# Fixing the issue order of ScalarE, VectorE and GpSimd in the attention stage of a fused gated-linear-attention and mixture-of-experts kernel

## The chip, the core and the metric

The kernel runs on one core of a Trainium2 chip. The metric is device time in microseconds of one execution; the quoted time before is the median of three runs. Engines are called PE (TensorE), ACT (ScalarE), DVE (VectorE), POOL (GpSimd) and SP (the queue that issues the DMAs). Each engine works through its own queue of instructions in the order in which they were put there.

## The reference

Two stages. The first is gated linear attention over 4 batches, 8 heads, 768 time steps, head dimension 48:

```python
for t in range(S):
    state = f[:, :, t, :, None] * state + einsum('bhd,bhe->bhde', k[:, :, t], v[:, :, t])
    y[:, :, t] = einsum('bhd,bhde->bhe', q[:, :, t], state)
```

with `f` the sigmoid of `f_logit`. Its output, reshaped to `x` of 3072 x 384, goes into a soft mixture of 8 experts: `P = exp(x @ w_gate - max)`, eight rounds of Sinkhorn (divide by row sums, then by column sums) over `P`, and `out = sum over e of P[:, e] * (relu(x @ w1[e]) @ w2[e])`, with `w1` 384 x 1024 and `w2` 1024 x 384 for each expert. All in float32.

## The kernel before

**Numbers.** Matmuls run in fp16 on split operands: each float32 operand is a high half and a low half, and three of the four products are kept. So each matmul is issued three times, and each evacuation has two parts: ACT writes the high half (`hh`, `xh`, `ah`, `sh`, `qh`, `vh`), then DVE or POOL subtracts it from the source and writes the low half (`hl`, `xl`, `al`, `sl`, `ql`, `vl`).

**Attention** is cut into 32 items: 4 batches x 2 halves of the sequence x 4 pairs of heads. One item covers 384 time steps in six chunks of 64. `pre(i)` (L398) loads `q3` (gates, q and k: one DMA, called `q<-in_qkf_dram` in the profile) and `vr`, takes the sigmoid (`ft`, ACT), runs two scans (`r` and `q`, DVE), scales and splits q and k (`kb`: high half on ACT, low half on POOL), and has SP transpose `kb` into `kt` by a DMA. `scores(i)` (L438) does the chunk scores (`aps`, 18 matmuls) and the key-value products (`kvps`, 18), masks and splits the scores (`am`, `ah`, `al`), and chains the states (`ut`, `sh`, `sl`). `outputs(i)` (L482) does `yps` (30 to 36 matmuls) and writes the fp16 pair `xh`, `xl`. After each fourth item `logits(u)` (L510) makes the gate logits of that 384-token unit `u`. Buffers limit how far items overlap: three of `q3`, two each of `kb`, `kt`, `vr`, `ut`, `ah`.

**Experts.** `moe(e, u)` (L317) does one expert for one unit: eight groups of nine `hps` matmuls, evacuated by `hh` and `hl`, then three groups of 24 `yps` matmuls. It is a generator that yields after each matmul, so it can fill PE's time elsewhere. `fill(n)` takes n expert matmuls from a list of 13 pairs (e, u) (`RAW`, 1872 matmuls), whose results `yr` are stored unscaled in DRAM and scaled later, when the Sinkhorn result is known. The loop over items (L600) puts 28 fills, then an item's `yps`, then 28 fills, then the next item's `aps` and `kvps`, from item 4 on: 56 fills for each item. The ten matmuls of Sinkhorn have 22 fills ahead of each. Everything left of the experts follows after that.

**What sets the order.** PE's order is the order of the calls: `mm` (L223) puts a dependency that carries no wait on the matmul before. The order on ACT, DVE, POOL and SP is made by the scheduler of the kernel's framework, which plays the program through with its own estimates of time and a priority; expert evacuations have the better priority `EPRIO`. Three scans are held back by hand (L412).

**PSUM.** Eight banks: three for the experts (`psm`), five for attention: one for `aps`, two for `kvps`, two for `yps`, the logits and Sinkhorn. After attention its five go to the experts (`bank`, L310). `guard` and `verdict` (L527, L564) reduce inputs and intermediates (`xmx`, `wmx`, `qkm`, `vm`) to a flag that tells whether the fp16 halves were wide enough.

Of the kernel before, what the change touches and what calls it, by code (L numbers as in the profile page):

```python
# [205 lines left out]
def fast(ctx, tc, qkf, vbd, wg, w1, w2, out, flag):  # L206
# [15 lines left out]

    def mm(transpose=False, **kw):  # L223
        ins = (nc.tensor.transpose if transpose else nc.tensor.matmul)(**kw)  # L224
# [10 lines left out]
    psm = ctx.enter_context(tc.tile_pool(name="psm", bufs=3, space=PSUM))  # L235
# [33 lines left out]
    def split_w(raw, e, j, k):  # L269
# [3 lines left out]
        if e < 2:  # L273
            nc.scalar.activation(out=raw, in_=raw, func=AF.Copy, scale=WS)
            nc.scalar.activation(out=wh, in_=raw, func=AF.Copy)
            nc.gpsimd.tensor_tensor(out=wl, in0=raw, in1=wh, op=ALU.subtract)
# [33 lines left out]
    def bank(shape, name):  # L310
        n = banks[0]
        banks[0] += 1
        if late and n % 8 >= 3:
            return late[1].tile(shape, F32, name=name, tag="m")
        return psm.tile(shape, F32, name=name, tag="m")

    def moe(e, u, w, mode):  # L317
# [3 lines left out]
        for f in range(FT):  # L321
# [15 lines left out]
            with at(EPRIO):  # L337
                nc.scalar.activation(out=th, in_=ps, func=AF.Relu)  # L338
                held[0] = nc.vector.scalar_tensor_tensor(out=tl, in0=ps, scalar=0.0, in1=th, op0=ALU.max, op1=ALU.subtract)  # L339
# [55 lines left out]
    done = {}  # L395
    tds = cst.tile([R, 32, NC], F32, name="tds")

    def pre(i):  # L398
# [8 lines left out]
        nc.scalar.activation(out=ft[:, 0:HS].rearrange("r (c t) -> r c t", t=C)[:, :, 1:C], in_=fl3[:, :, 1:C], func=AF.Sigmoid)  # L407
# [3 lines left out]
        scan = nc.vector.tensor_tensor_scan(out=r[:, ::-1], data0=ft[:, :0:-1], data1=ind[:, :0:-1], initial=0.0, op0=ALU.mult, op1=ALU.add)  # L411
# [4 lines left out]
        nc.vector.reciprocal(out=pi[:, :, 0], in_=pi[:, :, 0])
        nc.vector.tensor_tensor_scan(out=fl, data0=ft[:, 0:HS], data1=pi.rearrange("r c t -> r (c t)"), initial=0.0, op0=ALU.mult, op1=ALU.add)  # L417
        nc.gpsimd.tensor_tensor(out=td, in0=td, in1=r3[:, :, 0], op=ALU.mult)
        nc.gpsimd.tensor_tensor(out=fl, in0=fl, in1=q, op=ALU.mult)
# [3 lines left out]
        nc.vector.tensor_tensor(out=ql, in0=fl, in1=qh, op=ALU.subtract)  # L423
        km = k.rearrange("r (c t) -> r c t", t=C)
        nc.vector.scalar_tensor_tensor(out=km, in0=km, scalar=KS, in1=r3, op0=ALU.mult, op1=ALU.mult)
        for h in range(2):
            rs = slice(64 * h, 64 * h + D)
            cs = slice(64 * h, 64 * h + C)
            nc.scalar.activation(out=kb[rs, 0, :, cs], in_=km[rs], func=AF.Copy)  # L429
            nc.gpsimd.tensor_tensor(out=kb[rs, 1, :, cs], in0=km[rs], in1=kb[rs, 0, :, cs], op=ALU.subtract)  # L430
# [1 line left out]
        nc.sync.dma_start_transpose(out=kt, in_=kb.rearrange("r n c s -> r (n c) s"))
# [3 lines left out]
        return kb, kt, qh, ql, vh, vl, td

    def scores(i, st):  # L438
        b, hf, p = i // 8, (i // 4) % 2, i % 4
        kb, kt, qh, ql, vh, vl, td = st  # L440
        kh, kl = kb[:, 0], kb[:, 1]
        cs = [slice(c * C, (c + 1) * C) for c in range(NC)]
# [5 lines left out]
        ins = nc.vector.scalar_tensor_tensor(out=am, in0=aps, scalar=AS, in1=mask[:, None, :].to_broadcast([128, NC, C]), op0=ALU.mult, op1=ALU.mult)
# [17 lines left out]
        if hf:
            nc.gpsimd.tensor_scalar(out=ut[:, 0, :], in0=carry[p], scalar1=1.0, scalar2=1.0, op0=ALU.mult, op1=ALU.mult)
        for c in range(NC - hf):
            kv = kvps[c // 3][:, c % 3, :]
            un = ut[:, c + 1, :] if c < NC - 1 else carry[p]  # L470
            if hf or c:
                nc.vector.scalar_tensor_tensor(out=un, in0=ut[:, c, :], scalar=td[:, c:c + 1], in1=kv[0:R], op0=ALU.mult, op1=ALU.add)  # L472
            else:
# [2 lines left out]
        nc.gpsimd.tensor_tensor(out=ut[:, c0:], in0=ut[:, c0:], in1=td[:, c0:, None].to_broadcast([R, NC - c0, 96]), op=ALU.mult)
        nc.scalar.activation(out=sh[:, c0:], in_=ut[:, c0:], func=AF.Copy, scale=SS)  # L477
        nc.vector.scalar_tensor_tensor(out=sl[:, c0:], in0=ut[:, c0:], scalar=SS, in1=sh[:, c0:], op0=ALU.mult, op1=ALU.subtract)  # L478

        return ah, al, shw, slw, c0  # L480

    def outputs(i, st, sc):  # L482
# [20 lines left out]
        for si, so, kt in pcs:  # L503
            nc.scalar.activation(out=xh[so, kt, :], in_=yps[si], func=AF.Copy, scale=YS * XS)  # L504
# [185 lines left out]
```

## Time and profile before

| | |
|---|---|
| median of 3 runs | 1737.86 us (1737.3 to 1743.14) |
| profiled execution | 1742.68 us, of which its span is 1740.9 us |
| PE busy | 1622.4 us of the span |
| DVE, ACT, POOL busy | 794.9, 472.3, 213.1 us |
| mean granted PE clock | 0.983 |

A row of the profile names the line, the engine, the operation and `out<-in`. Lines are those of the kernel before; L224 is the helper through which every matmul goes, so matmuls are told apart by their tiles. A "busy" PE counts a matmul from its start to its modelled end, so neighbouring matmuls overlap in it. "PEclk" is the granted clock as a share of full speed.

### The profile page before, as it was taken

To read this page: it belongs to the slowest core of one execution; us is meant where nothing else is said; L and a number is where in the kernel's file an instruction comes from. 1 tells how busy PE (TensorE), PEld (TensorE's weight loads), DVE (VectorE), ACT (ScalarE), POOL (GpSimd) and SP (SyncE) were. 2 spreads that over 40 slices of the span, in tenths; PEclk is the share of its full clock that TensorE was granted. 3 is DMA by queue.
4 is the path that set the end of the run, shared out by engine and by line. 5 is a ranking of instruction groups with operands and counts; after the bars stand their busy time and mean duration, and the time that the engine had idled before them with its cause. 6 is when DMAs were issued, how large, how long until landed. Compare 5 with 4: busy or idle time off the path is not lost.

```text
span 1740.9 us, 27224 instructions
## 1 busy us (share of the span) xinstructions
PE 1622.4 (93%) x11566; PEld 1003.7 (58%) x11566; DVE 794.9 (46%) x1482; ACT 472.3 (27%) x947; POOL 213.1 (12%) x231
## 2 busy tenths in 40 slices
PE   2479898898999999999999999999999999999998
PEld 2246565565665566666666666666666666666665
DVE  8886666666468942235222522243223422223222
ACT  5544444444332221112111311122112211111111
POOL 7663343333100000000000000000000000000000
PEclk9989999999999999999999999999999999999999
DMA  8453343343014610002000200010000100000000
GB/s 196 129 141 99 95 100 96 97 115 74 27 51 159 171 37 1 1 10 64 1 1 1 73 1 1 1 47 27 1 1 19 37 1 1 1 5 24 28 29 29
DMA packets 87956, 86.72 MB, mean 50 GB/s; under 512 B 58768, under 2 KB 71952, under 8 KB 87824
## 3 DMA queue, kind: packets, MB, share of 16 engines
q1 hardware_dynamic: 87824, 84.89, 18.3%
q8 instruction: 92, 1.51, 0.4%
q14 instruction: 40, 0.33, 0.1%
HBM read 61.47 MB, written 12.39 MB: 42 GB/s over the span
## 4 chain that ended last, share of the span: by engine, by line
PE 75%; DVE 9%; DMA 7%; POOL 3%; issue 3%; ACT 2%; SPq 1%; POOLq 0%; ACTq 0%; DVEq 0%
PE yps L224 38%; PE hps L224 36%; DMA q<-in_qkf_dram 6%; DVE r L411 1%; POOL kb L430 1%; DVE hl L339 1%; DVE xl L506 1%; DMA yb<-ys 1%; DVE ql L423 1%; DVE wmx L285 1%; DVE q L417 1%; POOL al L454 1%; PE kvps L224 1%; ACT xh L504 1%; DVE vl L435 1%
## 5 line engine op out<-in xcount | busy, mean ns | idle before, releaser
L224 PE MATMUL yps<-w2h,hl 128*128 128x384 f16 x1536 | 501.4, 326 | 6.1 <-DVE hl L339 5.9
L224 PE MATMUL yps<-w2h,hh 128*128 128x384 f16 x1536 | 501.3, 326 | 4.5 <-DVE hl L339 4.5
L224 PE MATMUL yps<-w2l,hh 128*128 128x384 f16 x1536 | 501.3, 326 | 0.0
L338 ACT ACTIVATE hh<-hps 128x384 f16<-128x384 f32 x512 | 246.7, 488 | 911.2 <-PE hps L224 910.6
L224 PEld LDWEIGHTS <-w1h 128*128 128x128 f16 x3072 | 301.4, 98 | 240.4 <-issue 47.2
L339 DVE SCALAR_TENSOR_TENSOR hl<-hps,hh 128x384 f16<-128x384 f32 x512 | 280.2, 554 | 342.8 <-ACT hh L338 341.7
L224 PEld LDWEIGHTS <-hh 128*128 128x128 f16 x3072 | 300.3, 98 | 195.8 <-issue 1.0
L224 PE MATMUL hps<-xh,w1h 128*128 128x384 f16 x1536 | 339.4, 329 | 43.6 <-DVE hl L339 36.4
L224 PE MATMUL hps<-xh,w1l 128*128 128x384 f16 x1536 | 339.4, 330 | 0.0
L224 PE MATMUL hps<-xl,w1h 128*128 128x384 f16 x1536 | 337.9, 328 | 0.0
L306 DVE SCALAR_TENSOR_TENSOR acc<-yps,pes,acc 128x384 f32<-128x384 f32 x153 | 94.4, 617 | 430.4 <-PE yps L224 430.4
L224 PEld LDWEIGHTS <-hl 128*128 128x128 f16 x1536 | 150.5, 98 | 112.1 <-DVE hl L339 9.8
L224 PEld LDWEIGHTS <-w1l 128*128 128x128 f16 x1536 | 151.4, 99 | 101.4 <-issue 5.0
L430 POOL TENSOR_TENSOR kb<-q,kb 48x384 f16<-48x384 f32 x64 | 64.4, 1006 | 31.6 <-ACT kb L429 29.2
L224 PEld LDWEIGHTS <-kb 112*128 112x128 f16 x576 | 26.6, 110 | 45.5 <-issue 33.0
L411 DVE TENSOR_TENSOR_SCAN r<-ft,ind 112x384 f32<-112x384 f32 x32 | 33.1, 1038 | 37.4 <-ACT ft L407 37.3
L478 DVE SCALAR_TENSOR_TENSOR sl<-ut,sh 112x480 f16<-112x480 f32 (+1 forms) x32 | 25.4, 795 | 49.7 <-ACT sh L477 49.7
L224 PE MATMUL aps<-qh,kb 112*128 112x64 f16 x384 | 26.8, 211 | 22.9 <-ACT qh L422 22.9
L472 DVE SCALAR_TENSOR_TENSOR ut<-ut,tds,kvps 112x96 f32<-112x96 f32 x144 | 44.6, 310 | 5.2 <-PE kvps L224 0.2
L429 ACT ACTIVATE kb<-q 48x384 f16<-48x384 f32 x64 | 33.3, 520 | 49.8 <-PE aps L224 33.8
L224 PE MATMUL yps<-qh,sh 112*128 112x64 f16 x176 | 33.8, 202 | 9.2 <-ACT sh L477 9.2
L224 PE MATMUL yps<-qh,sl 112*128 112x64 f16 x176 | 33.7, 199 | 7.7 <-DVE sl L478 7.7
(130 smaller groups left out, 1118.3 us busy)
## 6 DMA issues: line engine op xcount, KB each, us to landing
q<-in_qkf_dram SPq DMA_DIRECT2D x32, 504.0 KB, 5.1
w1r<-in_w_dram SPq DMA_DIRECT2D x32, 384.0 KB, 3.5
w2r<-in_w_dram SPq DMA_DIRECT2D x32, 384.0 KB, 3.2
vr<-in_vbd_dram SPq DMA_DIRECT2D x32, 288.0 KB, 3.4
ys<-yr SPq DMA_DIRECT2D x39, 192.0 KB, 2.0
yb<-ys SPq DMA_DIRECT2D x13, 576.0 KB, 4.0
out_dram<-acc SPq DMA_DIRECT2D x24, 192.0 KB, 1.9
vs<-in_vbd_dram SPq DMA_DIRECT2D x4, 384.0 KB, 3.5
```

The lines of the kernel that those rows point to most:

```text
L224: ins = (nc.tensor.transpose if transpose else nc.tensor.matmul)(**kw)
L285: ins = nc.vector.tensor_reduce(out=wmx[:, k - 1, 4 * e + j:4 * e + j + 1], in_=wh.rearrange("p a f -> p (a f)"), axis=AX.X, op=ALU.max, a ...
L306: nc.vector.scalar_tensor_tensor(out=a, in0=y, scalar=p, in1=a, op0=ALU.mult, op1=ALU.add)
L338: nc.scalar.activation(out=th, in_=ps, func=AF.Relu)
L339: held[0] = nc.vector.scalar_tensor_tensor(out=tl, in0=ps, scalar=0.0, in1=th, op0=ALU.max, op1=ALU.subtract)
L411: scan = nc.vector.tensor_tensor_scan(out=r[:, ::-1], data0=ft[:, :0:-1], data1=ind[:, :0:-1], initial=0.0, op0=ALU.mult, op1=ALU.add)
L417: nc.vector.tensor_tensor_scan(out=fl, data0=ft[:, 0:HS], data1=pi.rearrange("r c t -> r (c t)"), initial=0.0, op0=ALU.mult, op1=ALU.add)
L423: nc.vector.tensor_tensor(out=ql, in0=fl, in1=qh, op=ALU.subtract)
L429: nc.scalar.activation(out=kb[rs, 0, :, cs], in_=km[rs], func=AF.Copy)
L430: nc.gpsimd.tensor_tensor(out=kb[rs, 1, :, cs], in0=km[rs], in1=kb[rs, 0, :, cs], op=ALU.subtract)
L472: nc.vector.scalar_tensor_tensor(out=un, in0=ut[:, c, :], scalar=td[:, c:c + 1], in1=kv[0:R], op0=ALU.mult, op1=ALU.add)
L478: nc.vector.scalar_tensor_tensor(out=sl[:, c0:], in0=ut[:, c0:], scalar=SS, in1=sh[:, c0:], op0=ALU.mult, op1=ALU.subtract)
```

## The change

The attention item becomes one generator, `item(i)`, in 25 stages. A loop counts steps `g`; at each step every live item runs one stage, oldest first, then a weight load may follow, then about nine fills (56 in six steps). A new item begins every six steps (`STEPS`), with six steps more (`GAP`) between items 3 and 4. Below, "step n of an item" counts from its sigmoid: 0 `ft`; 1 first scan and `vh`; 2 second scan and k; 3 `vl`, q on POOL, `kb` high; 4 `qh`, `kb` low; 5 the transpose; 6 `ql`; 8 `aps` and `kvps`; 9 `am`; 10 `ah` and half of `ut`; 11 the rest of `ut`, and `al`; 12 `ut` on POOL; 14 `sh`; 16 `sl`; 17 `yps`; 18 `xh`; 19 `xl`; and for each fourth item 22 to 25 the logits. The two loads stand four steps ahead of step 0.

`pin` ties each instruction of ACT, DVE and POOL to the one called before it on the same engine, with the same waitless dependency that PE has. It acts from step 24 until attention ends, on the items, on the weights of experts 0 and 1 and on the evacuations of the fills. SP is not pinned.

The experts get four PSUM banks (`psm`), attention four: `yps` has one bank, the logits share the bank of `aps`, Sinkhorn takes the `kvps` pair. Loads of expert weights stand at fixed steps: expert 0 at steps 16 to 30, expert 1 at 36 to 50. Fills begin at step 38, where item 4's `aps` stands, so 56 of them come ahead of item 5's `aps` where 28 did. `guard` becomes a generator that is called piece by piece during expert 3, and its `xmx` reductions are tied behind an expert evacuation.

```diff
+STEPS = 6
 FILL = 56
+GAP = 6
...
+    last, fixed = {}, [False]
+
+    def pin(ins):
+        engine = ins.ins.engine
+        if fixed[0]:
+            if engine in last:
+                behind(ins, last[engine])
+            last[engine] = ins
+        return ins
...
-    psm = ctx.enter_context(tc.tile_pool(name="psm", bufs=3, space=PSUM))
+    psm = ctx.enter_context(tc.tile_pool(name="psm", bufs=4, space=PSUM))
...
-        if late and n % 8 >= 3:
+        if late and n % 8 >= 4:
...
-                nc.scalar.activation(out=th, in_=ps, func=AF.Relu)
+                pin(nc.scalar.activation(out=th, in_=ps, func=AF.Relu))
...
-    def pre(i):
+    def item(i):
...
+        yield from wait(4)
+        pin(nc.scalar.activation(out=ft[:, 0:HS]..., func=AF.Sigmoid))
...
+            pin(nc.scalar.activation(out=kb[rs, 0, :, ks], in_=km[rs], func=AF.Copy))
+        yield
...
+            pin(nc.gpsimd.tensor_tensor(out=kb[rs, 1, :, ks], in0=km[rs], in1=kb[rs, 0, :, ks], op=ALU.subtract))
+        yield
...
         nc.sync.dma_start_transpose(out=kt, in_=kb.rearrange("r n c s -> r (n c) s"))
...
-        yps = psa.tile([128, HS], F32, name=f"yps_{i}", tag="y")
+        yps = psa.tile([128, HS], F32, name=f"yps_{i}", tag="y", bufs=1)
...
-        ps = psa.tile([128, HS], F32, name=f"lps{u}", tag="y")
+        ps = psa.tile([128, HS], F32, name=f"lps{u}", tag="a", bufs=1)
...
         for u in range(U):
-            nc.vector.tensor_reduce(out=xmx[:, u, :], in_=xt[u][0], axis=AX.X, op=ALU.max, ...)
+            yield
+            behind(nc.vector.tensor_reduce(out=xmx[:, u, :], in_=xt[u][0], axis=AX.X, op=ALU.max, ...), held[0])
...
+    loads = {}
     for j in range(4):
-        loads[6 + j // 2] = loads.get(6 + j // 2, []) + [(1, 1, j), (1, 2, j)]
+        loads[16 + 2 * j], loads[24 + 2 * j] = (0, 1, j), (0, 2, j)
+        loads[36 + 2 * j], loads[44 + 2 * j] = (1, 1, j), (1, 2, j)
+    begin = {STEPS * i + (GAP if i >= 4 else 0): i for i in range(4 * U)}
+    live, g, filling = [], -4, False
+    while live or g < max(begin):
+        fixed[0] = g >= STEPS * 4
+        if g + 4 in begin:
+            live.append(item(begin[g + 4]))
+        for it in list(live):
+            if next(it, it) is it:
+                live.remove(it)
+        if g in loads:
+            e, k, j = loads[g]
+            if len(ws[e][k - 1]) == j:
+                ws[e][k - 1].append((load_w1 if k == 1 else load_w2)(e, j))
+        if g >= STEPS * 3 + 20:
+            fill(FILL * (g % STEPS + 1) // STEPS - FILL * (g % STEPS) // STEPS)
+        g += 1
+    fixed[0] = False
-    late.append(ctx.enter_context(tc.tile_pool(name="psb", bufs=5, space=PSUM)))
+    late.append(ctx.enter_context(tc.tile_pool(name="psb", bufs=4, space=PSUM)))
+    checks = guard()
```

ACT in the middle of attention, before. `ft_113<-q_12` is the sigmoid of item 12, `kb_112<-q_10` the high half of k of item 10, `hh` are expert evacuations:

```order
L422 ACTIVATE qh_1667<-q_10_1654 112x384
L504 ACTIVATE xh_959<-yps_1406 96x384
L407 ACTIVATE ft_113<-q_12_2051 112x6x63
L409 ACTIVATE tds<-q_12_2051 112x6
L338 ACTIVATE hh_0_2_1473<-hps_0_2_1399 128x384
L338 ACTIVATE hh_0_3_1487<-hps_0_3_1477 128x384
L338 ACTIVATE hh_0_4_1501<-hps_0_4_1491 128x384
L429 ACTIVATE kb_112<-q_10_1654 48x6x64 x2
```

The same engine at the same place now:

```order
L442 ACTIVATE kb_118<-q_9_1378 48x6x64 x2
L372 ACTIVATE yr_0_0_1610<-yps_0_0_1531 128x384
L476 ACTIVATE ah_1618<-am_1597 128x384
L446 ACTIVATE qh_1624<-q_9_1378 112x384
L515 ACTIVATE xh_1042<-yps_1638 32x384 x3
L421 ACTIVATE ft_113<-q_10_1583 112x6x63
L423 ACTIVATE tds<-q_10_1583 112x6
```

Before, the sigmoid of item i+2 stood ahead of the k of item i; now an item's k stands ahead of the next item's sigmoid.

SP at that place, before. The first transpose is item 9's, the second item 10's:

```order
L432 DMA_TRANSPOSE kt_146<-kb_118 128x12x112
L402 DMA q_12_2051<-in_qkf_dram 112x1152
L404 DMA vr_1852<-in_vbd_dram 128x576
L432 DMA_TRANSPOSE kt_144<-kb_112 128x12x112
L402 DMA q_13_2242<-in_qkf_dram 112x1152
```

And now, from item 8's transpose to item 9's and the load behind it:

```order
L451 DMA_TRANSPOSE kt_144<-kb_112 128x12x112
L415 DMA q_11_1770<-in_qkf_dram 112x1152
L417 DMA vr_1772<-in_vbd_dram 128x576
L451 DMA_TRANSPOSE kt_146<-kb_118 128x12x112
L373 DMA ys_105<-yr_0_0_1610 128x384
L415 DMA q_12_1987<-in_qkf_dram 112x1152
```

In both, the load for item i+3 stands right behind the transpose of item i; what moved is ACT's sigmoid that uses it.

PE at the end of Sinkhorn, now. `sk_c` are its last two column sums, `yps_7_2` the last of the 1872 fills, `hps_3_0` the first matmul of the expert stage behind it:

```order
L236 LDWEIGHTS hh_7_7_6697
L236 MATMUL yps_7_2_6779<-w2l_3_639,hh_7_7_6697 128x384
L236 MATMUL sk_c_6798<-sk_cs,onesf 128x8
L236 MATMUL sk_c_6828<-sk_cs,onesf 128x8
L236 LDWEIGHTS w1h_0_710
L236 MATMUL hps_3_0_6849<-xh_2639,w1h_0_710 128x384
```

Before, its last column sum stood among fills:

```order
L224 LDWEIGHTS hl_7_6_6706
L224 MATMUL yps_7_1_6773<-w2h_3_1120,hl_7_6_6706 128x384
L224 MATMUL sk_c_6767<-sk_cs,onesf 128x8
L224 LDWEIGHTS hh_7_6_6705
L224 MATMUL yps_7_1_6773<-w2l_3_1121,hh_7_6_6705 128x384
```

The fills now run out earlier: 16 stand ahead of the last column sum but one, none ahead of the last.

More of the change, by code (lines that the diff above doesn't have):

```diff
@@ L416, in pre @@
[L416 to L419, printed above, removed]
+        pin(nc.vector.tensor_scalar(out=pi[:, :, 0], in0=r3[:, :, 0], scalar1=T_MIN, scalar2=None, op0=ALU.max))
+        pin(nc.vector.reciprocal(out=pi[:, :, 0], in_=pi[:, :, 0]))
@@ L423, in pre @@
[L423 to L430, printed above, removed]
+        pin(nc.scalar.activation(out=qh, in_=fl, func=AF.Copy))
@@ L436, in pre @@
[L436 to L440, printed above, removed]
+        yield
+        pin(nc.vector.tensor_tensor(out=ql, in0=fl, in1=qh, op=ALU.subtract))
+        yield from wait(2)
         kh, kl = kb[:, 0], kb[:, 1]
-        cs = [slice(c * C, (c + 1) * C) for c in range(NC)]
         aps = psa.tile([128, NC, C], F32, name=f"aps_{i}", tag="a", bufs=1)
@@ L503, in outputs @@
         for si, so, kt in pcs:
-            nc.scalar.activation(out=xh[so, kt, :], in_=yps[si], func=AF.Copy, scale=YS * XS)
+            pin(nc.scalar.activation(out=xh[so, kt, :], in_=yps[si], func=AF.Copy, scale=YS * XS))
+        yield
         for si, so, kt in pcs:
-            ins = nc.vector.scalar_tensor_tensor(out=xl[so, kt, :], in0=yps[si], scalar=YS * XS, in1=xh[so, kt, :], op0=ALU.mult, op1=ALU.subtract)
-        if i == 3:
-            done[5] = done[6] = ins
-    def logits(u):
-        xh, xl = xt[u]
-        fill(FILL // 4)
-        ps = psa.tile([128, HS], F32, name=f"lps{u}", tag="y")
+            pin(nc.vector.scalar_tensor_tensor(out=xl[so, kt, :], in0=yps[si], scalar=YS * XS, in1=xh[so, kt, :], op0=ALU.mult, op1=ALU.subtract))
+        if p < 3:
+            return
+        yield from wait(3)
+        ps = psa.tile([128, HS], F32, name=f"lps{u}", tag="a", bufs=1)
         n = 0
@@ L518, in logits, with wait @@
                 n += 1
+        yield
         lt = ap.tile([2 * NE, HS], F32, name=f"lt{u}", tag="am")
-        nc.scalar.activation(out=lt, in_=ps[0:2 * NE], func=AF.Copy, scale=1.0 / (XS * GS))
-        fill(FILL // 4)
-        ps2 = psa.tile([128, TT, 2 * NE], F32, name=f"lps2{u}", tag="y")
+        pin(nc.scalar.activation(out=lt, in_=ps[0:2 * NE], func=AF.Copy, scale=1.0 / (XS * GS)))
+        yield
+        ps2 = psa.tile([128, TT, 2 * NE], F32, name=f"lps2{u}", tag="a", bufs=1)
         for t in range(TT):
             mm(transpose=True, out=ps2[:, t, :], in_=lt[:, t * 128:(t + 1) * 128], identity=identf[0:2 * NE, 0:2 * NE])
-        nc.vector.tensor_reduce(out=lg[:, u * TT:(u + 1) * TT, :], in_=ps2.rearrange("p t (n e) -> p t e n", n=2), axis=AX.X, op=ALU.add)
+        yield
+        pin(nc.vector.tensor_reduce(out=lg[:, u * TT:(u + 1) * TT, :], in_=ps2.rearrange("p t (n e) -> p t e n", n=2), axis=AX.X, op=ALU.add))
+    def wait(n):
+        for _ in range(n):
+            yield
     def guard():
@@ L554, in guard @@
         for u in range(U):
-            nc.vector.tensor_reduce(out=xmx[:, u, :], in_=xt[u][0], axis=AX.X, op=ALU.max, apply_absolute_value=True)
+            yield
+            behind(nc.vector.tensor_reduce(out=xmx[:, u, :], in_=xt[u][0], axis=AX.X, op=ALU.max, apply_absolute_value=True), held[0])
+        yield
         nc.vector.tensor_reduce(out=g[:, 4:5], in_=xmx.rearrange("p u k -> p (u k)"), axis=AX.X, op=ALU.min)
@@ L642, in fast @@
                     largest(*early.pop(0))
-            if (e, u) == (3, 0):
-                guard()
+                if e == 3 and n % 24 == 12:
+                    next(checks, None)
+            if (e, u) == (3, U - 1):
+                for _ in checks:
+                    pass
             if (e, u) == (NE - 1, 1):
```

108 lines of the change are left out of this document (49 added, 59 removed).

## Prediction

> **What bounds the kernel now.** I read the page first, then a table of stretches, then the waits of the worst stretch, then one of its stalls in order of time.
>
> ```profile
> span 1740.9 us, 27224 instructions
> ```
>
> The stretches are the lead-in without fills, the first items with fills, steady attention, and (Sinkhorn and the start of the late experts left out) the rest. Columns: length, then busy us and instructions of PE, weight loads, DVE, ACT and POOL, then PE's granted clock, DMA share and GB/s.
>
> ```profile
> 0.00:67.60 67.60, 21.14 (x312) 19.44 (x313) 53.05 (x101) 35.63 (x68) 43.99 (x45) 1.00 0.75 183
> 67.60:120.30 52.70, 35.14 (x293) 21.31 (x293) 49.41 (x72) 31.43 (x58) 41.35 (x36) 0.84 0.49 121
> 120.30:452.00 331.70, 288.35 (x2976) 193.02 (x2975) 210.21 (x447) 146.06 (x321) 123.64 (x147) 0.95 0.39 96
> ...
> 620.00:1741.00 1121.00, 1115.09 (x6864) 671.29 (x6861) 355.41 (x601) 209.60 (x411) 0.00 (x0) 1.00 0.05 16
> ```
>
> From 620 us on PE is never idle except for the tail of 5.9 us, and the change leaves that part's work alone. What can be won lies before: PE is idle for 46.5, 17.6 and 43.4 us in the first three stretches, and in the second and third its clock is also cut, by 0.16 x 52.7 + 0.05 x 331.7 = 25 us of time. In steady attention no other engine is full (DVE 210 of 332 us, ACT 146, POOL 124), so PE waits for order, not for work. The waits of 120.3 to 452 us (total, times, longest):
>
> ```profile
> ACT ft L407 <- DMA q<-in_qkf_dram: 45.3, 19, 4.4
> ACT sh L477 <- POOL ut L476: 43.2, 19, 3.7
> DVE r L411 <- ACT ft L407: 34.5, 15, 3.6
> PE hps L224 <- DVE hl L339: 31.5, 10, 6.4
> ```
>
> PE itself waits for few things: mostly an expert bank whose `hl` is late. Behind that, ACT sits at the sigmoid of an item whose load has not landed, 19 times, and DVE at the scan behind it. One stall, in order of time:
>
> ```profile
> 201.52 1.37 SPq L432 DMA_TRANSPOSE kt<-kb  x1
> ...
> 203.62 0.68 ACT L477 ACTIVATE sh<-ut 112x576 f16<-112x576 f32 x1 [3.25 <-POOL ut L476]
> 203.87 0.38 SPq L402 DMA_DIRECT2D q<-in_qkf_dram  x1
> ...
> 206.83 0.49 ACT L338 ACTIVATE hh<-hps 128x384 f16<-128x384 f32 x1
> ...
> 208.18 0.52 ACT L407 ACTIVATE ft<-q 112x378 f32<-112x378 f32 x1 [0.86 <-DMA q<-in_qkf_dram]
> ```
>
> ```profile
> 210.53 0.48 PE L224 MATMUL hps<-xh,w1h 128*128 128x384 f16 x1 [6.42 <-DVE hl L339]
> ```
>
> ACT waits 3.25 us at `sh`, then does other attention rows; the expert's `hh` gets its turn only at 206.83, and PE has no bank for 6.42 us. The load is issued behind the transpose and used 4.3 us later.
>
> **The loop that the order makes.** The rows shown of ACT and SP before close a circle: the transpose of item i, then the load of i+3 behind it on SP, then its sigmoid on ACT, then, behind that on ACT, the k of item i+1, its low half on POOL, and the transpose of i+1. Its links:
>
> ```profile
> q<-in_qkf_dram SPq DMA_DIRECT2D x32, 504.0 KB, 5.1
> ```
>
> ```profile
> L407 ACT ACTIVATE ft<-q 112x378 f32<-112x378 f32 x20 | 10.4, 518 | 41.0 <-DMA q<-in_qkf_dram 40.9
> ```
>
> ```profile
> L429 ACT ACTIVATE kb<-q 48x384 f16<-48x384 f32 x44 | 22.9, 521 | 38.0 <-PE aps L224 29.3 <-issue 8.1
> ```
>
> ```profile
> L430 POOL TENSOR_TENSOR kb<-q,kb 48x384 f16<-48x384 f32 x44 | 41.5, 942 | 26.8 <-ACT kb L429 25.2
> ```
>
> That is 1.37 (issue of the transpose) + 5.1 + 0.52 + 0.52 + 2 x 0.94 = 9.4 us, plus up to three `hh` between sigmoid and k, each of which waits for its nine matmuls (1.46 us by the price below): 9.4 to 13.8 us an item. Now the prices of PE and the ends of the stage:
>
> ```profile
> 634.96 11.70 PE hps L224 x72
> ```
>
> ```profile
> 298.20:309.57 11.37, 11.37 (x126) 7.75 (x125) 5.99 (x14) 4.29 (x9) 5.15 (x7) 1.00 0.51 129
> ```
>
> ```profile
> 67.62 0.48 PE L224 MATMUL hps<-xh,w1h 128*128 128x384 f16 x1 [0.74 <-ACT xh L504]
> ```
>
> ```profile
> L448 DVE SCALAR_TENSOR_TENSOR am<-aps,mask x32: 525/548/559, 20.7 to 463.8; 128x384 f32<-128x384 f32 x32
> ```
>
> A fill costs 11.70 / 72 = 0.1625 us. From 298.20 to 309.57, the starts of two `aps`, PE runs a whole item with its 56 fills without a gap: 11.37 us, so the item's own matmuls cost 2.27. From the first fill to the last item's `am` are 396.2 us, in which PE has 1484 fills (241.2), 27 items (61.3) and seven logits of about 1.1 (7.7): 310 us of work. **86 us are lost there**, 61 of them idle and 25 to the clock; by the item that is 14.7 us for 11.4 of work.
>
> **The change, part by part.** *The loop is cut.* ACT now takes an item's k before the next sigmoid, and the load issued behind the transpose of item i (its step 5) is needed at its step 18, 13 steps later. A step is 9.3 fills, 1.5 us, so the 5.1 us of landing have 20 us of cover. The 45.3 us of ACT at the sigmoid go, and the 34.5 of DVE behind them. `sh` stands two steps after POOL's `ut`, so the 43.2 us go too, if POOL keeps up.
>
> *What is late next.* Loads for each item are 210.21 / 23 = 9.1 us on DVE (8.8 without `xmx`), 6.4 on ACT and 5.4 on POOL against PE's 11.4, so nothing is full, but DVE has little slack. Each engine now waits in a fixed place: `sl` (step 16) is queued behind the `hl` of step 15, and PE's `yps` (step 17) waits for it; behind `yps` stand all fills.
>
> ```profile
> L339 DVE SCALAR_TENSOR_TENSOR hl<-hps,hh 128x384 f16<-128x384 f32 x72 | 38.2, 546 | 9.4 <-ACT hh L338 9.0
> ```
>
> ```profile
> L478 DVE SCALAR_TENSOR_TENSOR sl<-ut,sh 112x576 f16<-112x576 f32 (+1 forms) x24 | 17.0, 708 | 49.3 <-ACT sh L477 49.3
> ```
>
> An `hl` ends about 1.1 us behind PE's step (0.49 of `hh` and 0.55), `sl` takes 0.7, and PE's next step gives 1.5, so `yps` waits 0.3 us at worst from that. [...] The same `ql` in two stretches (67.6 to 120.3, then 135 to 460), and POOL's weight rows that run in the first:
>
> ```profile
> L423 DVE TENSOR_TENSOR ql<-q,qh 112x384 f16<-112x384 f32 x5 | 9.1, 1842 | 0.0
> ```
>
> ```profile
> L423 DVE TENSOR_TENSOR ql<-q,qh 112x384 f16<-112x384 f32 x22 | 13.0, 590 | 0.0
> ```
>
> ```profile
> L276 POOL TENSOR_TENSOR w1l<-w1r,w1h 128x768 f16<-128x768 f32 x8 | 13.7, 1720 | 0.8 <-ACT w1h L275 0.8
> ```
>
> 1842 ns beside POOL rows of 1720, 590 otherwise: about a whole POOL row is added. I take one POOL row of k, 0.94 us, lost for each item; the bounds are 0 (PE's own gap-free item) and two such rows, 1.9. By the 590 alone there would be no loss, and the time 23 us lower. [...]
>
> *Expert 1's weights* (steps 36 to 50, eight loads) are pinned ahead of the `hh` of their steps. PE needs 16 steps, 30.3 us; DVE has 2.67 items x 8.8 = 23.5 us, plus up to 8 x 1.72 = 13.8 behind POOL, 37. I take 10 us lost (7 over PE's time, 3 for waits), bounds 4 and 18. Before, this work fell in the stretch with DVE at 49.4 of 52.7 us.
>
> *Lead-in.* Up to the first fill the same rows run on DVE (53 of 67.6 us busy), but item 4 now follows item 3 in place of running among its rows. I take 0; bounds -5 (idle DVE closed) and +8 (item 4's chain from sigmoid to transpose left bare).
>
> *Fourth expert bank.* PE may run three groups, 4.4 us, ahead of an `hl` where it could run two, 2.9. No price of its own: it is the cover for DVE's lag above. One `yps` bank is free by step 19 and needed at 23; the logits share `aps`'s bank with a step between each user. I take nothing for either.
>
> *`xmx`.* Eight rows leave attention for expert 3, where PE is never idle:
>
> ```profile
> L555 DVE TENSOR_REDUCE xmx<-xh 128x3 f32<-128x1152 f16 x8 | 10.8, 1349 | 0.2
> ```
>
> The 0.35 us an item are in the 8.8 above, and cost nothing there.
>
> *Sinkhorn.* Fills run out, since they begin earlier and there are 1872 in both. DVE's own chain of one round, with two `hl` inside:
>
> ```profile
> 514.10 0.15 DVE L92 TENSOR_SCALAR sk_cs<-sk_c 128x8 f32<-128x8 f32 x1
> ...
> 517.02 0.50 DVE L89 TENSOR_REDUCE sk_cs<-pe 128x8 f32<-128x192 f32 x1
> ```
>
> is 3.4 us. 16 fills cover 2.6 of the last round but one, none covers the last: 0.8 + 2.9 (without the two `hl`) is about 3.5 us of new idle PE; bounds 2.5 and 5.
>
> **Clock.** Around the stall above:
>
> ```profile
> 204.00:210.50 6.50, 0.12 (x1) 0.00 (x0) 5.55 (x9) 4.59 (x11) 0.71 (x1) 0.87 0.64 168
> 210.50:217.00 6.50, 6.46 (x53) 4.50 (x53) 5.08 (x13) 2.06 (x4) 2.28 (x3) 0.60 0.02 4
> ```
>
> The clock falls to 0.60 for the stretch behind it. I let all 25 us of clock loss go, since no stall of more than 2 us remains in my sum. [...]
>
> **Sum.** Lost after: 10 + 24.7 items (steps 52 to 200) x 0.94 = 33 of the 86. Gain 53, less 3.5: 49.5 us. The profiled execution took 1742.68 us, 1.8 over its span and 4.8 over the median; 1740.9 - 49.5 = 1691.4 of span, and against the median 1737.86 - 49.5 = **1688.4**.
>
> **Rivals.** *Collisions cost double.* If DVE loses two POOL rows an item (1.9 us) and the weight stretch 10, the loss is 57 and the time 1737.9 - 29 + 3.5 = 1712. For it: DVE at 80% of PE's time, the 1842 ns. Against: `ql` at 590 in steady attention, where POOL was as busy. *Nearly free.* Losses of 0.1 an item and 4 us: 1737.9 - 80 + 3.5 = 1662. *The weights eat it.* Weight rows pinned ahead of `hh` also wait for their DMA (two raw buffers); with 18 us there, 1.9 an item and 8 us of lead-in, the gain is 86 - 65 - 8 - 3.5 = 9.5: 1728, no change that counts from there on. *Slower: the transposes.* `kvps` (step 8) must have `kt`, eight steps after a sigmoid that is now tied to PE's progress. PE's eight steps last 8 x 1.5 + 2.3 = 14.4 us; sigmoid 0.52, two scans at the row of one,
>
> ```profile
> L417 DVE TENSOR_TENSOR_SCAN q<-ft,pi 112x384 f32<-112x384 f32 x20 | 19.5, 973 | 0.5
> ```
>
> 1.95, three smaller rows and the scaling of k at little more than a third scan, 1.2, `kb` 0.52 + 1.88, and the transpose,
>
> ```profile
> kt<-kb SPq DMA_TRANSPOSE x32, 3.5
> ```
>
> come to 9.6. If each of the five changes of engine waits 1.6 us behind rows of other items, `kt` lands 3.2 us late, PE stops at every `kvps`, and the loss is 10 + 24.7 x (3.2 + 0.94) = 112: 1768. It decides once an item loses 3.3 us in all. For it: DVE and ACT rows that start only behind `hh` or `hl`. Against: those trail PE by about 1 us, and PE's stop gives the chain time. That the pins do nothing is excluded by the rows of ACT shown.
>
> **Chances.** Forecast 0.55 (1672 to 1702 on its own), double collisions 0.20, nearly free 0.10, gain eaten 0.07, slower 0.08. A measurement of this kernel can tell about 0.5% from no change: 1729 to 1747. Faster 0.85, same 0.07, slower 0.08. The range, 1662 to 1728, holds the first two cases and most of the third.
>
> **Right or wrong.** Right: in steady attention ACT's wait at the sigmoid for its load is gone, `aps` starts come 12 to 13 us apart, and the last `am` starts near 415 us against 463.8 (28 more fills, 4.6 us, stand ahead of it now); PE has one idle of about 3 us at the last `sk_c`. Wrong: `ql` and `sl` above 1.2 us on average (collisions), PE waiting at `kvps` for a DMA (transposes), first fill after 75 us (lead-in), or ACT waiting for `w1r` or `w2r` (weights).

## The result, and the profile after

The changed kernel took 1682.68 us in the median (four runs, 1681.21 to 1683.65), the kernel before 1737.58 beside it: a ratio of 0.9678, 95% interval 0.9655 to 0.9701. 1688.4 had been forecast. The profiled execution took 1681.94 us.

```profile
span 1680.2 us, 27209 instructions
```

The items give marks that both kernels share. The table of stretches of the kernel before, cut at the first fill, at the `am` of item 8 and at that of item 31 (columns as in the prediction):

```profile
67.60:143.60 76.00, 50.69 (x442) 31.75 (x442) 63.29 (x99) 38.96 (x76) 48.36 (x44) 0.85 0.48 122
143.60:463.80 320.20, 284.61 (x2967) 190.75 (x2965) 201.73 (x431) 142.54 (x310) 118.69 (x141) 0.96 0.37 91
463.80:620.00 156.20, 150.87 (x992) 90.46 (x989) 121.42 (x252) 45.53 (x83) 2.06 (x2) 0.99 0.40 117
```

The same stretches of the changed kernel:

```profile
66.20:120.00 53.80, 50.83 (x494) 33.30 (x492) 46.65 (x80) 35.40 (x68) 39.02 (x38) 0.93 0.66 157
120.00:399.70 279.70, 272.08 (x2956) 183.51 (x2955) 222.07 (x445) 146.80 (x321) 141.65 (x149) 1.00 0.49 108
399.70:560.00 160.30, 149.29 (x959) 88.58 (x956) 118.45 (x245) 44.40 (x81) 2.06 (x2) 0.98 0.39 115
```

The first of the three holds 28 more fills than before (4.6 us) and the last 28 fewer. With that, the first gave 76.0 + 4.6 - 53.8 = 26.8 us, the second 40.5, and the third took 160.3 + 4.6 - 156.2 = 8.7 back. With 1.4 in the lead-in and 0.7 behind 560 us that is the 60.7 by which the spans differ. In the second stretch PE's idle time fell from 35.6 to 7.6 us and its clock went from 0.96 to 1.00. The medians lie 5.8 us closer than the spans, since the profiled execution of before was about 5 us over its median and that of the changed kernel 0.7 under.

Two waits of that stretch in the kernel before, against which the experiments below are measured (total us, times, longest):

```profile
ACT ft L407 <- DMA q<-in_qkf_dram: 38.2, 17, 4.1
PE hps L224 <- DVE hl L339: 28.3, 9, 6.4
```

What ACT waited for in the second stretch of the changed kernel:

```profile
ACT hh L350 <- PE hps L236: 52.7, 41, 3.0
ACT yr L372 <- issue: 23.8, 10, 3.7
ACT yr L372 <- PE yps L236: 23.3, 13, 3.6
```

The sigmoid's wait for its load and that of `sh` for `ut` (45.3 and 43.2 us in the prediction's somewhat longer stretch) have left the list. ACT now waits for PE, which is how it has to be when PE is the bound. What PE still waits for, from 66 to 400 us:

```profile
PE yps L236 <- DVE sl L495: 5.6, 7, 2.3
PE lps L236 <- DVE am L469: 4.3, 4, 2.0
PE kvps L236 <- DMA kt<-kb: 0.5, 1, 0.5
```

No `hps` waits for a bank any more; small waits for single attention rows on DVE have come in their place.

### The profile page after: what moved, and what is told of

The parts are those of the page before. It is cut to its first block, busy times and chain, and to the rows that moved or that the text cites. A ratio compares the mean times of both kernels' runs of the same rounds, so it can differ in the third digit from the quotient of the medians.

```text
span 1680.2 us, 27209 instructions
## 1 busy us (share of the span) xinstructions
PE 1607.3 (96%) x11566; PEld 995.1 (59%) x11566; DVE 805.3 (48%) x1482; ACT 474.6 (28%) x947; POOL 230.3 (14%) x231
## 4 chain that ended last, share of the span: by engine, by line
PE 86%; DVE 6%; DMA 2%; ACT 2%; issue 2%; POOL 1%; SPq 0%; POOLq 0%; DVEq 0%; ACTq 0%
PE yps L236 43%; PE hps L236 41%; DVE hl L351 1%; PE kvps L236 1%; DVE wmx L297 1%; PE aps L236 1%; PE lps L236 1%; DMA q<-in_qkf_dram 1%; DVE acc L318 1%; DMA w2r<-in_w_dram 1%; DMA yb<-ys 1%; ACT hh L350 1%; DVE vl L438 1%; POOL kb L448 0%; DMA kt<-kb 0%
## 5 line engine op out<-in xcount | busy, mean ns | idle before, releaser
L350 ACT ACTIVATE hh<-hps 128x384 f16<-128x384 f32 x512 | 250.3, 490 | 955.4 <-PE hps L236 954.0
L236 PE MATMUL hps<-xh,w1l 128*128 128x384 f16 x1536 | 335.4, 327 | 0.0
L448 POOL TENSOR_TENSOR kb<-q,kb 48x384 f16<-48x384 f32 x64 | 76.7, 1198 | 16.2 <-ACT kb L442 13.7
L236 PE MATMUL yps<-qh,sl 112*128 112x64 f16 x176 | 33.5, 198 | 13.3 <-DVE sl L495 13.2
L439 POOL TENSOR_TENSOR q<-q 112x384 f32<-112x384 f32 x32 | 39.5, 1234 | 34.6 <-DVE q L433 24.6
L491 POOL TENSOR_TENSOR ut<-ut,tds 112x480 f32<-112x480 f32 (+1 forms) x32 | 39.6, 1237 | 22.6 <-DVE ut L481 11.8
L372 ACT ACTIVATE yr<-yps 128x384 f32<-128x384 f32 x39 | 19.1, 491 | 77.1 <-PE yps L236 48.1
L290 ACT ACTIVATE w2h<-w2r 128x768 f16<-128x768 f32 x24 | 20.2, 843 | 69.9 <-PE yps L236 38.8
```

The costliest lines, as they stand in the source:

```text
L350: pin(nc.scalar.activation(out=th, in_=ps, func=AF.Relu))
L372: pin(nc.scalar.activation(out=yr, in_=ps, func=AF.Copy))
L439: pin(nc.gpsimd.tensor_tensor(out=fl, in0=fl, in1=q, op=ALU.mult))
L448: pin(nc.gpsimd.tensor_tensor(out=kb[rs, 1, :, ks], in0=km[rs], in1=kb[rs, 0, :, ks], op=ALU.subtract))
L491: pin(nc.gpsimd.tensor_tensor(out=ut[:, c0:], in0=ut[:, c0:], in1=td[:, c0:, None].to_broadcast([R, NC - c0, 96]), op=ALU.mult))
```

## The experiments

My theory was that the loop through ACT (load, sigmoid, k, transpose) had set the pace, and that ACT's place in the change cuts it. Rivals: the fourth bank did it; or the stages and the new calls did it, and the pins little; or no single edge helps, only the whole pinned order. All ratios are to runs of the kernel before on the same chip, with the 95% interval in brackets; the median of that kernel moved between 1737.2 and 1741.6 us from one set of runs to the next. The first fill came between 65.8 and 69.1 us in executions of the changed kernel and its variants with pins, so what lies under 3 us is read from the stretches between two items and not from a span.

**One edge, put into the kernel before.** An edge is one fixed order between two rows of an engine: here the sigmoid of an item behind the k of the item before it.

```diff
...
-        nc.scalar.activation(out=ft..., func=AF.Sigmoid)
+        sig = nc.scalar.activation(out=ft..., func=AF.Sigmoid)
+        if i >= 7:
+            behind(sig, high[i - 1])
...
-            nc.scalar.activation(out=kb[rs, 0, :, cs], in_=km[rs], func=AF.Copy)
+            high[i] = nc.scalar.activation(out=kb[rs, 0, :, cs], in_=km[rs], func=AF.Copy)
```

> The kernel before with one rule added: from item 7 on, ACT's sigmoid of an item stands behind the high half of k of the item before it. Banks, PE order, fills and the scheduler for the rest stay. Circle theory (the loop load, sigmoid, k, transpose sets the 14.7 us an item before): ACT's wait at the sigmoid for its load falls from 45.3 us to under 10, aps starts come about 12 to 13 us apart, and the time falls by 25 to 45 us, to 1693 to 1713. Bank theory (three expert banks do not cover the evacuations): under 10 us of gain, 1728 to 1738. Theory of the whole pinned order (one edge only moves the wait to another place): within 10 us of before, or slower.

1709.49 us, ratio 0.9825 (0.9794 to 0.9855). The stretch between the `am` of items 8 and 31, and two of its waits:

```profile
134.70:431.80 297.10, 278.24 (x2968) 186.15 (x2965) 230.73 (x441) 144.20 (x312) 144.43 (x144) 0.98 0.39 98
```

```profile
ACT kb L431 <- PE aps L224: 24.1, 13, 6.1
PE hps L224 <- DVE hl L339: 13.2, 11, 4.2
```

Of the sigmoid's 38.2 us of waiting for the load in this stretch, 4.9 are left (at the second, small sigmoid `tds`). The 320.2 us are 297.1, and PE's waits for a bank fell from 28.3 to 13.2. One order between two rows of one engine is worth over half of the whole gain: that the order of sigmoid and k costs this time is shown, and that it is not all is shown too.

**Which engine's pins?** In the changed kernel, first nothing pinned, then all but ACT, then ACT alone.

```diff
-        if fixed[0]:
+        if False:                                        # nothing pinned
+        if fixed[0] and engine != nc.scalar.engine:      # all but ACT
+        if fixed[0] and engine == nc.scalar.engine:      # ACT alone
```

> The changed kernel with pin doing nothing: steps, PE order, four banks, weight steps and fills stay, the scheduler orders ACT, DVE and POOL; in its order the sigmoid of item i+2 stands ahead of the k of item i again. Circle theory: the circle is back, ACT waits 30 us or more at the sigmoid for its load, 1715 to 1740. Bank theory and schedule theory (banks, or the order of the calls and of PE, brought the gain): 1680 to 1695.

1716.16 us, ratio 0.9862 (0.9833 to 0.9891). ACT at the sigmoid, with stages, calls, banks and PE order of the changed kernel:

```profile
ACT ft L421 <- DMA q<-in_qkf_dram: 34.9, 19, 3.3
```

> The changed kernel with DVE and POOL pinned and ACT left to the scheduler, which puts the sigmoid of item i+2 ahead of the k of item i again. If ACT's order is the cause, the circle is back: ACT waits 25 us or more at the sigmoid for its load, and the time is 1705 to 1740. If any one fixed engine would do, 1680 to 1695.

1710.36 us, ratio 0.983 (0.9801 to 0.9858). Here the scheduler put the small sigmoid `tds` first, and it has the wait:

```profile
ACT tds L423 <- DMA q<-in_qkf_dram: 36.3, 16, 4.0
```

> The changed kernel with pin on ACT alone; the scheduler orders DVE and POOL. If ACT's order is what matters (the circle runs through ACT), 1680 to 1692. If the order on DVE or POOL is needed as well, 1697 to 1720.

1682.99 us, ratio 0.9687 (0.9667 to 0.9707): all of the gain. Its two stretches up to the last `am`:

```profile
68.30:128.90 60.60, 52.55 (x493) 33.89 (x492) 48.95 (x81) 36.01 (x70) 39.62 (x35) 0.90 0.56 143
```

```profile
128.90:400.50 271.60, 269.71 (x2946) 182.69 (x2944) 208.57 (x442) 144.59 (x319) 135.55 (x149) 1.00 0.48 111
```

Without ACT's pins the loop comes back and, by the ratios, 26 to 32 us are lost; with them alone the time is the same as with all. Not all of that loss is the loop's: between items 8 and 31 the two kernels without ACT's pins take 298.2 (nothing pinned) and 299.5 us (all but ACT), 18.5 and 19.8 more than the changed one. Of the rest, the kernel with nothing pinned loses 10.2 us ahead of the first fill (76.5 us), the other 13.9 in the stretch with expert 1's weights (67.7 us). The order on DVE and POOL only moves loss about: it is worth 6.8 us where expert 1's weights are loaded (60.6 against 53.8) and costs 8.1 in steady attention (279.7 against 271.6).

**The fourth bank.** Taken out of the changed kernel (the diff), put into the kernel before, and put there together with the edge.

```diff
-    psm = ctx.enter_context(tc.tile_pool(name="psm", bufs=4, space=PSUM))
+    psm = ctx.enter_context(tc.tile_pool(name="psm", bufs=3, space=PSUM))
...
-        yps = psa.tile([128, HS], F32, name=f"yps_{i}", tag="y", bufs=1)
+        yps = psa.tile([128, HS], F32, name=f"yps_{i}", tag="y")
...
```

> The changed kernel with three expert banks during attention and two for yps; pins and steps stay. Circle theory: PE loses a little at hps behind hl, 0 to 10 us in all, 1683 to 1693. Bank theory: most of the gain goes, 1715 to 1735.

1682.15 us, ratio 0.9662 (0.9636 to 0.9687). With three banks, PE's wait for one is

```profile
PE hps L236 <- DVE hl L351: 0.5, 1, 0.5
```

> The kernel before with only the fourth expert bank: psm 4, one yps bank, logits in the bank of aps, Sinkhorn in the kvps pair, four banks for the late experts. ACT's order is nearly unchanged. Circle theory: PE follows the circle at the same pace, 1728 to 1742. Bank theory: PE no longer waits for hl (31.5 us before) and the time falls to 1690 to 1710.

1718.99 us, ratio 0.9869 (0.9841 to 0.9897): outside what either theory gave. The stretch between items 8 and 31, and its waits at the sigmoid and for a bank:

```profile
142.60:439.20 296.60, 277.82 (x2941) 184.16 (x2940) 198.77 (x433) 139.65 (x308) 119.48 (x141) 0.97 0.41 98
```

```profile
ACT ft L407 <- DMA q<-in_qkf_dram: 33.3, 18, 3.3
PE hps L224 <- DVE hl L339: 14.8, 6, 5.8
```

The loop is still there (33.3 us of ACT against 38.2), yet PE runs 23.6 us faster, at 12.9 us an item in place of 13.9. So the loop has no fixed pace that PE must follow. By the waits, PE lost where a waiting ACT row held a `hh` back for longer than the banks could cover, and one bank more covers part of that. Whether the loop still sets the 12.9 is open: it lies inside the 9.4 to 13.8 us that I had given it, and the two kernels without ACT's pins, which have four banks and the loop too, take 13.0 an item although PE waits in them for other rows. With all but ACT pinned it waits for no bank there; it waits for `am`, 6.0 us, and

```profile
PE yps L236 <- DVE sl L495: 15.4, 11, 2.3
```

> The kernel before with both single parts: the sigmoid behind the k of the item before on ACT, and the fourth expert bank. Alone they gave 32 and 23 us in the last runs. If they take away two different losses, they add up: 1683 to 1692. If both only treat the same loss (ACT stopped at the sigmoid while `hh` stands behind it: the edge takes the stop away, the bank covers it), the two together give little more than the larger: 1700 to 1710. The bank added nothing to the pinned kernel, which speaks for the second.

1688.78 us, ratio 0.9712 (0.9691 to 0.9733): the gains add (1.75% and 1.31% alone, 2.88% together). The stretch and PE's wait for a bank:

```profile
132.80:408.80 276.00, 271.85 (x2967) 183.60 (x2964) 225.53 (x441) 144.09 (x312) 143.76 (x144) 1.00 0.42 105
```

```profile
PE hps L224 <- DVE hl L339: 3.0, 2, 1.5
```

28.3 us of waiting for a bank, 13.2 with the edge, 14.8 with the bank, 3.0 with both. So the second theory, that both treat one loss, is out. A likely reason is that the edge leaves ACT another stop, at `sh` for POOL's `ut` (52.9 us in this stretch, with the edge alone as with both): the four longest waits for a bank that are left with the edge alone, over 10 of the 13.2 us, end 4 to 8 us behind such a stop. Which stop caused which wait was not shown. With both edits those 52.9 us are still there and PE loses almost nothing: the second wait on the prediction's list did not have to go. In steady attention this kernel of two small edits is even 3.7 us quicker than the changed one (276.0 against 279.7). What it lacks is the stretch ahead, 66.8 us with 28 fewer fills, where `aps` of one item waited 10.7 us for its `qh` and then 5.4 for its `ql`: what the stages, the gap before item 4 and the earlier fills bring there was not taken apart. With ACT pinned, PE waits for a bank once at most, and the fourth bank is worth nothing.

**The wait at `sl`.** I had charged the meeting of `sl` with POOL's low half of k (steps 16 and 4 of two items fall together); moving `sl` a step ahead should show it.

```diff
         pin(nc.scalar.activation(out=sh[:, c0:], in_=ut[:, c0:], func=AF.Copy, scale=SS))
-        yield from wait(2)
+        yield
         pin(nc.vector.scalar_tensor_tensor(out=sl[:, c0:], ...))
-        yield
+        yield from wait(2)
```

> The changed kernel with `sl` in step 15 in place of 16, out of the step in which POOL writes the low half of k. In the changed kernel `sl` takes 1.13 us on average in steady attention (0.71 before) and PE's `yps` waits for it 13.2 us in all. If the meeting with POOL in one step and the short way to `yps` cost that, the wait falls below 4 us and the time by 5 to 10 us, to 1673 to 1678. If `sl` only meets another POOL row, or DVE stands behind `hl` anyway, within 3 us of the changed kernel, 1680 to 1686.

1686.57 us (1685.68 to 1689.2), ratio 0.9709 (0.9691 to 0.9727): no gain, and rather a loss (every run above every run of the changed kernel). PE's waits from 69 to 408 us:

```profile
PE lps L236 <- DVE am L469: 9.4, 4, 3.4
PE kvps L236 <- DMA kt<-kb: 3.4, 2, 2.8
PE yps L236 <- DVE sl L495: 0.8, 1, 0.8
```

The wait at `sl` went, as expected, but only to `am` and `kt`. Order of time at one item:

```profile
299.39 0.56 DVE L351 SCALAR_TENSOR_TENSOR hl<-hps,hh 128x384 f16<-128x384 f32 x1 [2.84 <-ACT hh L350]
299.84 2.30 POOL L448 TENSOR_TENSOR kb<-q,kb 48x384 f16<-48x384 f32 x2 [2.44 <-ACT kb L442]
299.86 1.50 DVE L495 SCALAR_TENSOR_TENSOR sl<-ut,sh 112x576 f16<-112x576 f32 x1
301.28 0.55 DVE L469 SCALAR_TENSOR_TENSOR am<-aps,mask 128x384 f32<-128x384 f32 x1
```

`sl` still meets POOL, and takes 1.50 us. But see the first line: DVE had stood idle for 2.84 us behind a `hl` that waited for PE's next group. In this item the crowd starts at that row; whether that is the rule, the next run shows better.

**Pins on DVE and POOL only while they help**, and the logits away from the bank of `aps`, and fewer fills for each Sinkhorn step.

```diff
-    last, fixed = {}, [False]
+    last, fixed = {}, [False, True]
...
-        if fixed[0]:
+        if fixed[0] and (engine == nc.scalar.engine or fixed[1]):    # DVE and POOL until step 54
...
-        fixed[0] = g >= STEPS * 4
+        fixed[0], fixed[1] = g >= STEPS * 4, g < STEPS * 9
...
-        ps = psa.tile([128, HS], F32, name=f"lps{u}", tag="a", bufs=1)
+        ps = psa.tile([128, HS], F32, name=f"lps{u}", tag="y")       # the same for ps2; with three expert banks
...
-SK_FILL = 22
+SK_FILL = 19
```

> The changed kernel with ACT pinned all through, DVE and POOL only until step 54, behind the loads of expert 1's weights. If the fixed places of DVE and POOL help in the weight stretch (idle PE 3.0 us with all pinned, 8.1 with ACT alone) and cost in steady attention (7.8 against 2.0), both gains are kept: 1674 to 1678. If the two only trade places, since PE ends up at the same point, 1680 to 1685.

1678.1 us, ratio 0.9649 (0.9624 to 0.9674). Item 8's `am` starts 54.5 us behind the first fill (53.8 with all pinned, 60.6 with ACT alone), and the way to item 31's is

```profile
123.50:395.10 271.60, 269.71 (x2945) 182.66 (x2944) 208.57 (x442) 144.56 (x319) 135.55 (x149) 1.00 0.47 110
```

so both gains are kept, 7.4 us from the first fill to the last `am` in the traces; the interval overlaps that of the changed kernel. DVE's waits for `hh` show where the 8.1 us between items 8 and 31 come from. In the changed kernel from 106 to 387 us, then here from 108 to 385 us:

```profile
DVE hl L351 <- ACT hh L350: 34.7, 30, 4.9
```

```profile
DVE hl L351 <- ACT hh L350: 19.8, 14, 3.0
```

In fixed order `am` stood behind such a `hl`; left free, it starts when `aps` is done. The same item in the two kernels, changed kernel first:

```profile
289.19 0.19 PE L236 MATMUL aps<-ql,kb 112*128 112x64 f16 x1
...
292.17 0.56 DVE L351 SCALAR_TENSOR_TENSOR hl<-hps,hh 128x384 f16<-128x384 f32 x1 [2.84 <-ACT hh L350]
292.65 0.55 DVE L469 SCALAR_TENSOR_TENSOR am<-aps,mask 128x384 f32<-128x384 f32 x1
...
294.54 1.00 DVE L495 SCALAR_TENSOR_TENSOR sl<-ut,sh 112x576 f16<-112x576 f32 x1
```

```profile
289.18 0.19 PE L236 MATMUL aps<-ql,kb 112*128 112x64 f16 x1
...
289.49 0.56 DVE L469 SCALAR_TENSOR_TENSOR am<-aps,mask 128x384 f32<-128x384 f32 x1
...
290.19 0.90 DVE L495 SCALAR_TENSOR_TENSOR sl<-ut,sh 112x576 f16<-112x576 f32 x1
...
292.34 0.55 DVE L351 SCALAR_TENSOR_TENSOR hl<-hps,hh 128x384 f16<-128x384 f32 x1
```

`am` starts 3.2 us sooner and `sl` 4.4.

> The changed kernel with three expert banks and two yps banks (no loss against four in an earlier run), and the logits in the yps banks in place of the bank of aps. If PE's 4.3 us of waiting at the logits for `am` comes from the shared bank, that wait goes and the time falls by 3 to 5 us against 1682, to 1677 to 1680. If the logits are late for another reason (their `xl`), the wait stays with another name: 1681 to 1684.

1680.14 us, ratio 0.9657 (0.9633 to 0.9681), against 0.9662 with the three banks alone: no gain to be seen. The wait at the logits went, but the next rows on the list grew, `yps` for `sl` from 5.6 to 8.3 us (66 to 400 us in both). By these waits the shared bank was only where DVE's lateness showed.

> The changed kernel with 19 fills ahead of each Sinkhorn matmul in place of 22, so that the last column sum has fills ahead of it again. If the 3.0 us of idle PE at the last column sum is lost time and 19 fills cover DVE's chain, 1678 to 1681. If the chain is longer than 19 fills (3.1 us), the idle time is only spread over the rounds: 1681 to 1684.

1678.37 us, ratio 0.966 (0.9641 to 0.9679). The stretch behind the last `am` shrank from 160.3 to

```profile
401.80:560.00 158.20, 149.20 (x967) 88.56 (x965) 118.74 (x247) 44.60 (x82) 2.06 (x2) 0.99 0.40 116
```

although it ends a little later in the program (8 more matmuls, 1.3 us): 3.4 us, the idle last round and its clock, less gaps of up to 0.7 in other rounds.

> The three edits together: 19 fills ahead of each Sinkhorn matmul (1678.4 alone), logits in the yps banks with three expert banks, and DVE and POOL pinned only until step 54. If they take away separate idle times of PE (3, 4 and 6 us), 1666 to 1672. If hybrid and logits treat the same waits of DVE, 1671 to 1676.

1674.64 us (five runs, 1671.35 to 1678.34), ratio 0.963 (0.9604 to 0.9656): the quickest version found, every run of it under every run of the changed kernel, though the two intervals touch. By the medians the three give 8.0 us together and 4.6, 2.5 and 4.3 alone, but each of these is known to about 4 us either way: whether they add in full, or the first two treat the same lateness of DVE, was not shown.

## Why the prediction was right, point by point

**The loop and its cure: right, in a form that was too simple.** ACT's wait at the sigmoid went, and undoing ACT's order alone brings it back. But I gave the loop as PE's pace, 9.4 to 13.8 us an item, and with the fourth bank alone PE went from 13.9 to 12.9 through the same loop. In the kernel before, all of PE's 35.6 us of idle time in steady attention are waits for expert evacuations, 28.3 of them for a bank, and the one edge takes more than half of these 28.3: there the loss was in `hh` rows kept waiting. With four banks and ACT unpinned, PE waits for attention rows as well, and how the loop reaches PE there stays open. The stall that I showed was not ACT's alone either: its `hh` ended at 207.32, and its `hl` began at 209.92, behind

```profile
206.83 1.69 DVE L506 SCALAR_TENSOR_TENSOR xl<-yps,xh 32x384 f16<-32x384 f32 x3 [0.54 <-ACT xh L504]
208.54 1.35 DVE L555 TENSOR_REDUCE xmx<-xh 128x3 f32<-128x1152 f16 x1
```

so 2.6 of the 6.42 us belong to DVE's order. The change moves `xmx` away; the kernel with edge and bank leaves it there and still takes 276.0 us.

**The fourth bank: right for this kernel** (no price, and none was found), by a reason that the runs corrected. I called it cover for DVE's lag. In the kernel before it covers ACT's stops, by the waits above, and in the changed kernel hardly any are left to cover.

**The loss that stays: right in kind, mis-sized; 33 us forecast, 18.7 measured.** From the first fill (66.3) to the last `am` (399.7) are 333.4 us for 1512 fills (245.7), 27 items (61.3) and seven logits (7.7). The weight stretch lost about 7 where I took 10. The term that was mis-sized is the 0.94 us an item for the meeting with POOL: 23 items took 279.7 us for 23 x 11.37 + 6 x 1.1 = 268.1 of work, 0.50 an item. The rows did get longer, in the changed kernel from 120 to 399.7 us:

```profile
L448 POOL TENSOR_TENSOR kb<-q,kb 48x384 f16<-48x384 f32 x46 | 54.6, 1187 | 13.9 <-ACT kb L442 12.1
L495 DVE SCALAR_TENSOR_TENSOR sl<-ut,sh 112x480 f16<-112x480 f32 (+1 forms) x23 | 26.1, 1135 | 0.0
L438 DVE SCALAR_TENSOR_TENSOR vl<-vr,vh 128x576 f16<-128x576 f32 x23 | 24.3, 1055 | 0.0
```

from 942, 706 and 751 ns in the kernel before, 0.73 us an item on these two rows of DVE alone. My error was to put DVE's longer rows down as PE's loss one for one: DVE is busy for 222.1 of 279.7 us, and takes most of it in time that it would have waited. That PE waits at all comes as much from the order: `am` behind a `hl` that isn't due yet. That an item loses a whole POOL row of k, as the sum has it, no run shows; the rows show this: `sl` took 0.75 us at 315.30, where POOL ran nothing, and 1.46 us at 121.45, beside two of POOL's `kb` rows. A scan (`r`, 0.96 us in the median) took 2.05 us from 78.81, beside a POOL row that ran from 78.41 to 80.05. But `hl` took no more than 0.56 us beside POOL rows, and of the five `ql` behind the prediction's 1842 ns, which took 0.54 to 3.10 us, one of 0.54 us (at 110.23) had a POOL row beside it all the while. What decides whether a DVE row grows, and by how much, was not shown.

**Lead-in: right** (0 forecast, 1.4 us gained, inside the spread of single executions).

**Clock: right in attention, wrong behind it.** In the second stretch, where 0.05 of the clock had been lost, it is 1.00; in the first it rose from 0.85 to 0.93 only. I had let all of that loss go since no stall of more than 2 us remained in my sum, though the last Sinkhorn round was one. It left PE idle for 2.96 us (3.5 in the sum), and the stretches around it are

```profile
465.00:469.30 4.30, 0.78 (x4) 0.61 (x5) 3.03 (x12) 0.49 (x1) 0.00 (x0) 1.00 0.12 46
469.30:475.00 5.70, 5.69 (x25) 2.99 (x25) 4.70 (x14) 1.38 (x3) 0.00 (x0) 0.70 0.32 105
```

0.30 x 5.7 = 1.7 us, which the sum does not have. That stalls of up to 2 us leave the clock alone was my own estimate, and no run shows it: in the kernel before, a clock of 0.51 came with gaps of 1.62 us and less (last section). The rest of the 8 us behind the last `am` (3.5 were forecast) is in the first late expert, where PE waited 6.6 us for `hl` (4.6 in the kernel before), and in the clock behind the longest of those waits (0.66 for 5.0 us, last section).

**The rivals.** Transposes that come too late cost 0.5 us at `kvps`. ACT waited for a weight's load once behind the first fill, for 2.8 us. Collisions at double the price were off by a factor of four. The nearest rival was the one of nearly free collisions: the second stretch, at 0.50 us an item, was between it (0.1) and the forecast (0.94).

**Signs.** `aps` starts came 12.2 us apart on average (12 to 13 forecast). The last `am` was 15 us earlier than the 415 that I gave, by the 14 us of loss that did not come; the 5 us more lost behind it, and the profiled execution of before being slower than its median, bring 67.3 of gain down to the 55 of the medians, 5.5 more than forecast. That the forecast came so close is thus in part luck: errors of 14 us one way and of 5 and 5 the other. The sign of collisions, `ql` or `sl` above 1.2 us on average, did not come, but `sl` at 1.135 missed it narrowly (`ql` 0.623).

## What to carry to other kernels

Look on the engine that empties the bottleneck's buffers for a row that waits ahead of such an evacuation: an order between two rows there can be worth more than a buffer, and here the buffer only covered what the order did wrong. Fix the order on that engine. On an engine that takes input from several sources, a fixed order can make it wait for rows that aren't due: here that of DVE and POOL cost 8.1 us where DVE had slack, and was worth 6.8 where DVE was busy for 46.65 of 53.8 us. When a row gets slower on an engine with idle time, price the wait of the one who needs its result, not the added duration.

## What was not expected of the hardware

The clock was also below 1 behind shorter idle times than the 2.96 us above. In the changed kernel PE's idle time of 2.39 us up to 540.25 (a `yps` waiting for its `hl`) was followed by

```profile
540.00:545.00 5.00, 4.75 (x19) 2.41 (x20) 5.00 (x8) 0.00 (x0) 0.00 (x0) 0.66 0.33 109
```

while two gaps of 1.34 and 0.79 us, up to 487.28 and 488.74, came with a clock of 1.00:

```profile
486.00:492.00 6.00, 3.92 (x24) 2.18 (x25) 6.00 (x10) 0.84 (x1) 0.00 (x0) 1.00 0.72 230
```

By the row, the gap of 2.39 us cost 0.34 x 5.0 = 1.7 us more than its own length. It had another gap of 0.71 us three microseconds ahead of it, but a single gap came with a lower clock too: in the kernel before with the fourth bank, PE was idle for 2.30 us up to 551.20, with no other wait from 538 to 556 us, and then

```profile
551.10:554.60 3.50, 3.40 (x11) 1.59 (x12) 3.50 (x7) 0.84 (x1) 0.00 (x0) 0.51 0.42 66
```

Nor was there always one gap as long as these: in the kernel before, gaps of 0.41, 1.62 and 1.53 us, the last of them up to 601.84, came with a clock of 0.51 from 601.3 to 604.8 us. The price was not the same each time either. Behind the same last Sinkhorn round, with 2.95 us idle, the kernel with ACT alone pinned shows

```profile
469.10:476.00 6.90, 5.84 (x19) 2.99 (x20) 5.58 (x17) 0.69 (x2) 0.00 (x0) 0.51 0.22 72
```

which is 0.49 x 6.9 = 3.4 us where the changed kernel lost 1.7. What decides between the two was not found.
